# A banded attention, a SiLU feed-forward and a top-1 expert stage in one kernel: five small edits to the order of its work

## The chip, the cores and the metric

The kernel runs on one core of one Trainium2 chip. A core has TensorE (PE, with its weight loads shown apart as PEld), VectorE (DVE), ScalarE (ACT), GpSimd (POOL) and SyncE (SP, which here issues nearly all of the transfers). Each engine works through its own list of instructions in the order in which they stand, and waits where an instruction needs something that isn't there yet. The metric is the device time of one execution in microseconds (us); the figure that counts is the median of several runs.

## The reference

Three parts follow each other. Inputs are drawn at random; there are 2 x 768 = 1536 tokens of width 512.

```python
# attention: 2 batches, 8 heads, 768 positions, head width 64
scores = q @ k.T / 8 + bias            # bias = -slope[h] * distance
keep   = (col < n_global) | ((row - col >= 0) & (row - col < n_local))   # 8 and 96
a      = softmax(where(keep, scores, -1e9))
x      = a @ v                         # [1536, 512]
# feed-forward, width 2048
h = x @ w_in;  x = (h * sigmoid(h)) @ w_out
# experts: 8 of them, width 1024; each token goes to the one with the largest logit
e   = argmax(x @ w_gate)
out = softmax(..)[e] * sigmoid(x @ w_output_gate)[e] * (relu(x @ w1[e]) @ w2[e])
```

## The kernel before, in words

**Attention.** The tokens stand in 12 tiles of 128, and a slot `s` is one tile and one pair of heads (`n,hp=divmod(s,4)`). In the first 24 slots (`slot_b`, tiles 0 to 5) the scores of slot `s+1` are computed on PE (`emit_qk`, L174, tile `xy`), DVE adds the distance table `tabs` and takes the extreme (`emit_tb`, L184), ACT takes the exponential (L195), PE transposes the result (L214), DVE or ACT copies it out (L220), and PE multiplies it by v (`emit_px`, L231, tile `px`). After the four slots of a tile the reciprocal sums are spread over 512 columns (`rx`), turned on PE into a bank `rb` (`emit_rb`, L238), copied from there to `xn` by DVE (L242) and multiplied into `px` (L243); POOL then writes `xT`. The distance tables come from three DVE steps in `table` (L124, L125, L126) over columns 0 to 2 or column 3, and from `tab_heads` (L129, L130). Before the first scores PE runs idle products on a constant tile (`warm`, L84), four before the two limits `n_global` and `n_local` are spread by a small product (`spread`, L92) and four behind it.

**The second half of the attention** (`slot`, tiles 6 to 11) is interleaved with the feed-forward. It splits the exponentials into two half-precision parts; the lower part is a subtraction (`emit_l`, L202, tile `hl`), given to POOL for the head pairs in `LOPB` and to DVE for the one that isn't in it. In the slot with `hp==1` POOL also splits the tile's v (L154), and the lower part of head pair 0 is computed in that same slot.

**Feed-forward.** Two token groups `u` of 256 are done in the first pass (`c==0`), then one at a time. Each step `f` of 16 does `s1_mm` (L356, 12 products of 256 columns for a group), the activation on ACT and DVE (L360, L362, L365, L366), and, two steps late, `s2_mm` (L377 to L379). In the first pass each step also decodes and splits the weights for later steps: L304, L305, L306 on DVE, L328 on ACT, L334 and L340 on POOL. `s2_mm` of step 0 takes the four accumulator banks `s20` to `s23`, which until then were handed round by `abank`, for `rb` among others.

**Experts.** Each expert `p` has 8 steps `f`: `f1_mm` (L716, L717 or L722), `f1_ev`, some splits of the next expert's weights (`split_u`, L586 on ACT and L587 on DVE), and `f2_mm` two steps late (L744 to L751). The rows of the next expert are turned by `prep_x` (L706 on PE into `xm`, L708 on ACT and L709 on DVE into `xwT`), one tile of up to 128 rows a step, from step `PX=4` on; the second expert has three such tiles. `tail` (L697, L698) copies the factor and the token number of a row.

What sets the order is the code itself: `manual_schedule` keeps the instructions of each engine as they are written, and the rotation of banks and buffers adds the waits.

Of the kernel before, what the change touches and what calls it, by code (L numbers as in the profile page):

```python
# [10 lines left out]
F32 = mybir.dt.float32  # L11
# [5 lines left out]
AF = mybir.ActivationFunctionType  # L17
ALU = mybir.AluOpType
AX = mybir.AxisListType
P = 128  # L20
# [3 lines left out]
def kernel(ctx, tc, qk, v, n_global, n_local, w_in, w_out, wg, w1, w2, out):  # L24
# [6 lines left out]
    SB=24  # L31
# [4 lines left out]
    LS=3  # L36
    WL=6
    DQS=(9,10,11,13,15,17,18,19,21)
    LOPB=(1,2,3)
    WPL=(4,6,8,10,12,14,16,18,20)  # L40
    WPS=(12,18,22)
    const=ctx.enter_context(tc.tile_pool(name="const",bufs=1,side="left"))
# [1 line left out]
    attn=es_a.enter_context(tc.tile_pool(name="attn",bufs=1,side="right"))  # L44
# [29 lines left out]
    V=nc.vector; A=nc.scalar; G=nc.gpsimd; T=nc.tensor; S=nc.sync  # L74
# [6 lines left out]
    def warm(k):  # L81

        if not wm: wm.append(ps.tile([P,512],F32,tag="s1b",name="wm",bufs=1))
        for _ in range(k): T.matmul(wm[0].rearrange("p (a b) -> p a b",a=4),ones,ones[:,None,:].to_broadcast([P,4,P]),start=True,stop=True)  # L84
# [34 lines left out]
    def table(k,steps=(0,1,2)):  # L119

        w=tabm['w'][0]
        rel,col,loc,a=(w[:,i,k] for i in range(4))
        ng=pf[:,0:1]; nl=pf[:,2:3]
        if 0 in steps: V.tensor_scalar(out=loc,in0=rel,scalar1=nl,scalar2=BIG,op0=ALU.is_ge,op1=ALU.mult)  # L124
        if 1 in steps: V.scalar_tensor_tensor(out=loc,in0=col,scalar=ng,in1=loc,op0=ALU.is_ge,op1=ALU.mult)  # L125
        if 2 in steps: V.scalar_tensor_tensor(out=a,in0=rel,scalar=nl,in1=loc,op0=ALU.min,op1=ALU.add)  # L126
# [6 lines left out]
    def abank(shape,name):  # L133
        tg=atags[0][acnt[0]%len(atags[0])] if not ded[0] else 'a'; acnt[0]+=1
        return ps.tile(shape,F32,tag=tg,name=name,bufs=1)
# [64 lines left out]
    def emit_l(n,hp):  # L200
        t=tt.pop((n,hp)); x=hl.pop((n,hp)); nch=ce=1 if n%NT==0 else 2
        (G if hp in LOPB else V).tensor_tensor(out=x[:,:,1],in0=t[:,:,:ce],in1=x[:,:,0],op=ALU.subtract)  # L202
        y=attn.tile([P,2,2,nch,P],F16,tag="pT",name="pT",bufs=3)
# [29 lines left out]
    rb={}  # L233
    def emit_rb(n):

        r=rs.pop(n)
        m=abank([P,KC,P],"rb")
        for k in range(KC): T.transpose(m[:,k,:],r[:,k*P:(k+1)*P],ident)  # L238
        rb[n]=m
    def emit_xx(n):  # L240
        m=rb.pop(n); x=attn.tile([P,KC,P],F32,tag="t",name="xn",bufs=3)
        V.tensor_copy(x,m)  # L242
        V.tensor_tensor(out=x,in0=pvt[n],in1=x,op=ALU.mult)  # L243
        put_xt(n,x,G)
    def emit_pv(n,hp):
# [28 lines left out]
    def put_xt(n,m,e=None):  # L274
        c,u=divmod(n,2)
        if u==0: xT[c]=mp.tile([P,2,KC,256],F32R,tag="xT",name="xT",bufs=3)
        sl=xT[c][:,:,:,u*P:(u+1)*P]
        if e: e.tensor_copy(sl[:,0],m)
        else: A.activation(out=sl[:,0],in_=m,func=AF.Copy)
        (e or V).tensor_tensor(out=sl[:,1],in0=m,in1=sl[:,0],op=ALU.subtract)  # L280
# [341 lines left out]
    def late_split():  # L622
        xr=xrp[NTT//2-1]
        for t in range(2): ea['l',t]=halves(xr[:,t,:512],(G,V)[t])
# [21 lines left out]
    def early1(hf,part):  # L646
        if part==0: ea['t']=s1bank([P,512],"eh")
        t=ea['t']; x=ea['xT']
        for k in range(6*part,6*part+6):
            ww,xx=((0,0),(0,1),(1,0))[k//4]; kc=k%4  # L650
            T.matmul(t,x[:,xx,kc,:],uq[2*hf,kc][:,ww],start=(k==0),stop=(k==11))
        if part==0: return
        h=m2['a'].tile([P,512],F32,tag="eh",name="ehs",bufs=2); ea['h',hf]=h
        A.activation(out=h,in_=t,func=AF.Relu)
# [116 lines left out]
    def folds():  # L771
        while late: late.pop(0)()
# [12 lines left out]
    def moe2():  # L785
        late_split()
        early1(0,0)
        run_gates(2)
        early1(0,1)
        logits(NTT-2)  # L790
        early1(1,0)
        run_gates(1)
        late1()
        run_gates(1)
        early1(1,1)
        run_gates(1)
        early2(0)
        late3()
        order(1)
        moe2_open2()  # L800
        for k in range(NQR):
            load_u(4+k//4,k%4)
            if k==3: load_x(1)
        load_t(0)
        early3(0,0)
        early2(1)
        early3(0,1); early3(1,0)
        early3(1,1)
        early4()
        atags[0]=['s1','s1b','a','pv']  # L810
        LG=2
        steps=[(p,f) for p in range(NE) for f in range(8)]
        for g in range(len(steps)+LG):
            if g<len(steps):
                p,f=steps[g]
                def spl():
                    split_u(4*(p+1)+nq[1]//4,nq[1]%4,False); nq[1]+=1
                f1_mm(p,f)
                if f!=2: folds()
                if p+1<NE and f==0: nq[:]=[0 if p else NQR,0]  # L820
                ns=(0,0,3,3,3,3,2,2)[f] if p+1<NE else 0
                f1_ev(p,f,spl if ns else lambda: None)
                if p+1==NE and 2<=f<5: flags(f-2)
                if p+1<NE:
                    for _ in range(ns-1): spl()
                    while nq[0]<min(16,nq[1]+4*(f+1),nq[1]+NQR): load_u(4*(p+1)+nq[0]//4,nq[0]%4); nq[0]+=1
                    if p and f==0: load_x(p+1)
                    if p==0 and f==5:
                        for k,s,n in tiles(0): tail(0,k,xwt[0][:,k,0:1],xwt[0][:,k,1:2])
                    t=tiles(p+1)  # L830
                    px=PX
                    if px<=f<px+len(t): prep_x(p+1,t[f-px][0])
            if g>=LG:
                p2,f2=steps[g-LG]
                if p2<NE-1:
                    f2_mm(p2,f2)
                    if f2==7: f2_ev(p2)
                    continue
                big,last=tiles(p2)
                if f2==7: f2_mm(p2,0,[big])  # L840
                f2_mm(p2,f2,[last])
                if f2==7:
                    f2_ev(p2,[last])
                    for k in range(1,8):
                        f2_mm(p2,k,[big])
                        if k==2: folds()
                    f2_ev(p2,[big])
# [156 lines left out]
    def slot_b(s):  # L1004

        ev=[]
        n5,h5=divmod(s-LT-2,4); o5=0<=s-LT-2<SB
        n,hp=divmod(s,4); n1,h1=divmod(s-1,4); n3,h3=divmod(s-LT,4); n4,h4=divmod(s-LT-1,4)
        n2,h2=divmod(s-2,4); cur=s<SB; o1=0<=s-1<SB; o2=0<=s-2<SB; o3=0<=s-LT<SB; o4=0<=s-LT-1<SB
        def a_():  # L1010
            if s<SB-3: want(min(s+WL,SB-1))
            elif cur: want(s+3)
            if s==0:
                m=two()
                for j in range(2): emit_qk(n,hp,j,m)
            if cur: emit_tb(n,hp,0)
            if s+1<SB or o3: m=two()
            if o3: cp[0]=emit_tr(n3,h3,m)
            if s+1<SB:
                for j in range(2): emit_qk(*divmod(s+1,4),j,m)  # L1020
            if s<3: warm(2)
            if s>=SB and o3: emit_cp(*cp[0],V)
            if o1 and s<SB: emit_exp(n1,h1)
        ev.append(a_)
        def a2():
            if cur: emit_tb(n,hp,1)
            if o3 and s<SB: emit_cp(*cp[0],A if DQ<=s<23 else V)
            if o1 and s>=SB: emit_exp(n1,h1)
            if o4: emit_px(n4,h4)
            if o3 and h3==3 and own(n3): emit_rb(n3)  # L1030
            if o4 and h4==3 and not own(n4): emit_rb(n4)
            if o5 and h5==3 and not own(n5): emit_xx(n5)
            if o2 and h2==3:
                for k in range(2): emit_rs(n2,k)
                r=attn.tile([P,512],F32,tag="t",name="rx",bufs=3)
                G.tensor_copy(r.rearrange("p (h d) -> p h d",h=H),rs[n2].to_broadcast([P,H,D])); rs[n2]=r
        ev.append(a2)
        def b_():
            if cur: glob_k(n,hp)
            if h4==3 and o4 and own(n4): emit_xx(n4)  # L1040
            if s==0: table(slice(0,3),(1,))
            if s==1: table(slice(0,3),(2,))
            for d,h in TB.get(s,()): tab_heads(slice(0,2) if d==0 else slice(2,3),slice(0,2) if d==0 else slice(2,3),(h,))
            if hp==3 and 4*(n+1)<SB and cur: load_v(n+1)
        ev.append(b_)
        return ev
    cp=[None]
# [41 lines left out]
    with tc.manual_schedule():  # L1089
# [3 lines left out]
        warm(4)  # L1093
        table_floats(slice(3,4),V)
        spread()
        warm(4)
        table(slice(3,4))
        table_floats(slice(0,3),A)
        tab_heads(slice(3,4),slice(3,4),range(H))
        table(slice(0,3),(0,))  # L1100
        rows_init()
        s=0
        while s<SB:
# [12 lines left out]
        def run_gates(k):  # L1116
            for _ in range(min(k,len(gq))): gq.pop(0)()
        for g in range(len(steps)+LAG):
            live=g<len(steps)
            if live:  # L1120
                c,f=steps[g]
# [116 lines left out]
```

## Time and profile before

| | us |
|---|---|
| median of 3 runs | 564.19 (563.9 to 564.52) |
| profiled execution, its own time | 564.78 |
| span of the profiled execution | 563.0 |
| PE busy | 548.8 |
| DVE busy | 385.9 |
| ACT busy | 309.9 |
| POOL busy | 168.5 |

The span runs from the first to the last instruction, and 1.8 us of the profiled execution's time lie around it. Busy time says how long an engine had an instruction in work; a wait of PE shows as a hole in its rows, and in brackets behind the instruction that ends the hole stands its length and what released it. The chain of waits goes back from the last instruction to whatever released each step. A matmul row merges equal instructions that follow each other (x12: twelve of them), and its duration runs to the modelled end of the last, so that two rows that follow each other are better compared by their starts.

### The profile page before, as it was taken

The page shows a single profiled execution, that of the slowest core. Times are in us where ns is not written, and L with a number is a line of the kernel's source. Part 1 is how long each engine was busy: PE and PEld are TensorE (multiplying, and loading weights), DVE is VectorE, ACT ScalarE, POOL GpSimd, SP SyncE. Part 2 cuts the span into 40 slices and gives each one's busy share as a digit, 9 for nine tenths or more (in the row PEclk, how much of TensorE's full clock was granted, in tenths as well). Part 3 has the DMA queues.
Part 4 walks back from the last instruction along what each step waited for, and adds up shares of the span by engine and source line. Part 5 has one row for each costly group of instructions (what it writes and reads, how often), then busy time and mean ns, then how long its engine had stood idle before and what let it go on. Part 6 is the DMA issues. An engine that isn't in the chain of part 4 may idle for free.

```text
span 563.0 us, 12050 instructions
## 1 busy us (share of the span) xinstructions
PE 548.8 (97%) x4051; PEld 467.9 (83%) x4051; DVE 385.9 (69%) x1115; ACT 309.9 (55%) x823; POOL 168.5 (30%) x231
## 2 busy tenths in 40 slices
PE   8999899999999999999999999999999999999993
PEld 4668799998888888888999989889887888888881
DVE  6997888884588857565634458548674966977950
ACT  6993444442645565444623436627655776867740
POOL 4875977765141521232101010210011010010011
PEclk9999999999999999999999999999999999999997
DMA  7870887895575875854594259129673866867500
GB/s 224 280 252 17 297 264 238 259 315 177 180 177 143 189 195 138 194 154 124 119 179 128 80 161 368 72 74 349 218 223 134 269 219 225 263 215 270 159 20 23
DMA packets 87531, 106.76 MB, mean 190 GB/s; under 512 B 35980, under 2 KB 50316, under 8 KB 87460
## 3 DMA queue, kind: packets, MB, share of 16 engines
q1 hardware_dynamic: 84980, 99.25, 59.4%
q0 software_dynamic: 2192, 6.39, 3.0%
q8 instruction: 34, 0.56, 0.4%
q10 hardware_dynamic: 288, 0.26, 0.2%
q14 instruction: 37, 0.30, 0.2%
HBM read 87.14 MB, written 17.66 MB: 186 GB/s over the span
## 4 chain that ended last, share of the span: by engine, by line
PE 86%; DVE 6%; DMA 2%; ACT 2%; issue 1%; SPq 1%; POOL 0%; POOLq 0%; DVEq 0%; ACTq 0%
PE s L356 23%; PE s L377 8%; PE s L378 7%; PE s L379 7%; PE h L716 6%; PE y L749 4%; PE y L750 4%; PE y L751 4%; PE h L717 4%; PE xy L174 3%; PE pv L255 2%; PE h L722 2%; PE y L745 1%; PE y L744 1%; PE px L231 1%
## 5 line engine op out<-in xcount | busy, mean ns | idle before, releaser
L356 PE MATMUL s<-xT,wi 128*128 128x256 f32 x1152 | 152.5, 284 | 0.0
L356 PEld LDWEIGHTS s<-xT,wi 128*128 128x128 f32 x1152 | 147.2, 190 | 5.4 <-issue 0.3
L360 ACT ACTIVATE u<-s 128x256 f32<-128x256 f32 x96 | 36.4, 380 | 96.2 <-PE s L356 92.8
L377 PE MATMUL s<-woh,g 128*128 128x512 f32 x192 | 78.5, 409 | 1.6 <-DVE xn L242 1.6
L587 DVE TENSOR_TENSOR uq<-qr,uq 128x512 fp32r<-128x512 f32 x112 | 74.3, 689 | 3.1 <-ACT uq L586 1.1
L378 PE MATMUL s<-woh,g 128*128 128x512 f32 x192 | 75.7, 394 | 0.0
L586 ACT ACTIVATE uq<-qr 128x512 fp32r<-128x512 f32 x112 | 66.5, 625 | 0.7 <-DMA qr<-in_w_dram 0.7
L673 POOL DMA_INDIRECT out_dram<-y,ixt x17 | 18.9, 1111 | 155.6 <-ACT y L762 115.8
L362 DVE SCALAR_TENSOR_TENSOR s<-u,s 128x256 f32<-128x256 f32 x64 | 27.2, 425 | 54.7 <-ACT u L360 54.6
L195 ACT ACTIVATE t<-t,mx 128x256 f32<-128x256 f32 (+1 forms) x96 | 46.0, 485 | 0.5 <-DVE mx L184 0.5
L377 PEld LDWEIGHTS s<-woh,g 128*128 128x128 f32 x192 | 36.3, 189 | 8.8 <-DVE xn L242 2.0
L202 POOL TENSOR_TENSOR hl<-t,hl 128x512 f16<-128x512 f32 (+1 forms) x18 | 19.6, 1088 | 73.6 <-ACT g L365 32.1
L378 PEld LDWEIGHTS s<-woh,g 128*128 128x128 f32 x192 | 36.3, 189 | 5.0
L379 PE MATMUL s<-wolr,g 128*128 128x512 f32 x128 | 39.8, 392 | 0.0
L366 DVE TENSOR_TENSOR g<-s,g 128x256 fp32r<-128x256 f32 x64 | 26.9, 421 | 16.6 <-ACT g L365 14.8
L729 DVE TENSOR_TENSOR h<-h,hs 128x192 f32<-128x192 f32 (+5 forms) x56 | 20.8, 372 | 25.3 <-ACT hs L728 25.3
L365 ACT ACTIVATE g<-s 128x256 fp32r<-128x256 f32 x64 | 24.2, 378 | 23.0 <-DVE s L362 22.9
L749 PE MATMUL y<-uq,hh 128*128 128x512 f32 (+1 forms) x88 | 36.7, 417 | 0.0
L750 PE MATMUL y<-uq,hh 128*128 128x512 f32 (+1 forms) x88 | 34.6, 394 | 0.0
L751 PE MATMUL y<-uq,hh 128*128 128x512 f32 (+1 forms) x88 | 34.6, 393 | 0.0
L731 ACT ACTIVATE hh<-h 128x192 fp32r<-128x192 f32 (+5 forms) x56 | 19.7, 352 | 26.3 <-DVE h L729 15.8
L716 PE MATMUL h<-xwT,uq 128*128 128x448 f32 (+5 forms) x144 | 32.5, 347 | 0.0
(282 smaller groups left out, 1106.2 us busy)
## 6 DMA issues: line engine op xcount, KB each, us to landing
qr<-in_w_dram SPq DMA_DIRECT2D x128, 256.0 KB, 4.1
wolr<-wlo_d SPq DMA_DIRECT2D x64, 256.0 KB, 3.3
wiraw<-in_w_in_dram SPq DMA_DIRECT2D x16, 512.0 KB, 5.1
wraw<-in_w_out_dram SPq DMA_DIRECT2D x13, 512.0 KB, 3.7
ring<-in_qk_dram SPq DMA_DIRECT2D x22, 256.0 KB, 4.3
xe<-xe SPq DMA_DIRECT2D x7, 792.0 KB, 5.8
wlo_d<-wol SPq DMA_DIRECT2D x16, 256.0 KB, 2.9
xw<-xe SPq DMA_DIRECT2D x15, 264.0 KB, 4.7
```

Of the source, the lines that this page charges most:

```text
L195: A.activation(out=t[:,j,:ce],in_=t[:,j,:ce],func=AF.Exp,scale=-1.0 if 4*n<SB else 0.125,bias=mx[n][:,h:h+1],accum_out=ss[n][:,h,0:1])
L356: T.matmul(t,w[:,ww,kc,:],x[:,xx,kc,:],start=(k==0),stop=(k==11)); k+=1
L360: A.activation(out=u,in_=t,func=AF.Tanh,scale=0.5)
L377: T.matmul(o,g[u][:,0,sl],wh,start=(f==0),stop=False)
L378: T.matmul(o,g[u][:,1,sl],wh,start=False,stop=False)
L379: else: T.matmul(o,g[u][:,0,sl],wl,start=False,stop=(f==FB-1))
L586: A.activation(out=t[:,0],in_=r,func=AF.Copy)
L587: (G if (i%2 if pool is None else pool) else V).tensor_tensor(out=t[:,1],in0=r,in1=t[:,0],op=ALU.subtract)
L716: for kc in range(KC): T.matmul(t[:,:2*W],uq[4*p+2*(f//4),kc][:,0,s],xwT[p,kc][:,:,:W],start=(kc==0),stop=False)
L749: T.matmul(o,hi,w[:,0],start=(f==0),stop=False)
L750: T.matmul(o,g[:,z:z+n],w[:,0],start=False,stop=False)
L751: T.matmul(o,hi,w[:,1],start=False,stop=(f==7))
```

## The change

Five edits. The second run of idle products has one product where it had four. The first step of the tables of columns 0 to 2 (L124) moves from the place ahead of the first slot to the place behind the first slot's two score instructions. The copy of `rb` into `xn` for the last tile of the first half (tile 5) is done by ACT, and stands right behind the turns that fill `rb`; the other tiles keep theirs on DVE where it was. The lower parts of head pair 0 go to POOL and those of head pair 2 to DVE (`LOPB`). The second expert's rows are turned one step sooner, at steps 3, 4 and 5 of the first expert, and the two `tail` calls of the first expert move from step 5 to step 7.

```diff
-    LOPB=(1,2,3)
+    LOPB=(0,1,3)
...
         for k in range(KC): T.transpose(m[:,k,:],r[:,k*P:(k+1)*P],ident)
         rb[n]=m
+        if n==SB//4-1: rb_copy(n,A)
+    def rb_copy(n,e):
+        m=rb[n]; x=rb[n]=attn.tile([P,KC,P],F32,tag="t",name="xn",bufs=3)
+        if e is V: V.tensor_copy(x,m)
+        else: A.activation(out=x,in_=m,func=AF.Copy)
     def emit_xx(n):
-        m=rb.pop(n); x=attn.tile([P,KC,P],F32,tag="t",name="xn",bufs=3)
-        V.tensor_copy(x,m)
+        if n<SB//4-1: rb_copy(n,V)
+        x=rb.pop(n)
         V.tensor_tensor(out=x,in0=pvt[n],in1=x,op=ALU.mult)
         put_xt(n,x,G)
...
-                    if p==0 and f==5:
+                    if p==0 and f==7:
                         for k,s,n in tiles(0): tail(0,k,xwt[0][:,k,0:1],xwt[0][:,k,1:2])
                     t=tiles(p+1)
-                    px=PX
+                    px=PX if p else PX-1
                     if px<=f<px+len(t): prep_x(p+1,t[f-px][0])
...
-            if s==0: table(slice(0,3),(1,))
+            if s==0: table(slice(0,3),(0,1))
...
         spread()
-        warm(4)
+        warm(1)
         table(slice(3,4))
         table_floats(slice(0,3),A)
         tab_heads(slice(3,4),slice(3,4),range(H))
-        table(slice(0,3),(0,))
         rows_init()
```

On DVE at the program's start, from the tables of column 3 (`wk`) to the first scores of head pair 0 (L184, two instructions each with the read of the extreme into `mx`), this stood before:

```order
L126 SCALAR_TENSOR_TENSOR wk<-wk,pf 128x128
L129 TENSOR_SCALAR tabs<-wk 128x128 x2
L124 TENSOR_SCALAR wk<-wk,pf 128x384
L181 MEMSET ss 128x8
L184 ISA t,mx<-xy,tabs 128x128
L184 ISA mx 128x1
L125 SCALAR_TENSOR_TENSOR wk<-wk,pf 128x384
```

and this stands there now:

```order
L126 SCALAR_TENSOR_TENSOR wk<-wk,pf 128x128
L129 TENSOR_SCALAR tabs<-wk 128x128 x2
L181 MEMSET ss 128x8
L184 ISA t,mx<-xy,tabs 128x128
L184 ISA mx 128x1
L124 TENSOR_SCALAR wk<-wk,pf 128x384
L125 SCALAR_TENSOR_TENSOR wk<-wk,pf 128x384
```

The two score instructions of the first head pair (the second one and its read are left out in both) have moved ahead of the 384-column step.

On ACT around feed-forward step 1 (the activations of `s_950` and `s_963` are its two groups, `woh` and `wi` are weight parts for later products) this stood before:

```order
L360 ACTIVATE u<-s_950 128x256
L360 ACTIVATE u<-s_963 128x256
L365 ACTIVATE g<-u 128x256 x2
L328 ACTIVATE woh<-wt 128x512
L328 ACTIVATE wi<-wt 128x512
```

and this stands there now (the lines of the changed program are five higher):

```order
L365 ACTIVATE u<-s_947 128x256
L365 ACTIVATE u<-s_960 128x256
L370 ACTIVATE g<-u 128x256 x2
L244 ACTIVATE xn<-rb 128x512
L333 ACTIVATE woh<-wt 128x512
L333 ACTIVATE wi<-wt 128x512
```

The copy of `rb` stands between the step's activations and the next weight parts; on DVE the copy L242 is gone from its place behind a decode (L306) of the following step.

On ACT in steps 3 and 4 of the first expert (`uq` are split weights of the second expert, `xwT` its turned rows) this stood before:

```order
L728 ACTIVATE hs<-h_5614 128x192
L586 ACTIVATE uq<-qr 128x512
L731 ACTIVATE hh<-h_5614 128x192
L586 ACTIVATE uq<-qr 128x512 x2
L708 ACTIVATE xwT<-xm 128x4x128
L728 ACTIVATE hs<-h_5658 128x192
```

and this stands there now:

```order
L736 ACTIVATE hh<-h_5575 128x192
L591 ACTIVATE uq<-qr 128x512 x2
L713 ACTIVATE xwT<-xm 128x4x128
L733 ACTIVATE hs<-h_5621 128x192
L591 ACTIVATE uq<-qr 128x512
L736 ACTIVATE hh<-h_5621 128x192
```

`h_5614` and `h_5621` are the same step 4 in the two programs, and the first tile of turned rows stands ahead of its activations where it stood behind them.

## Rows read from the trace of the kernel before

**Rows 1.** Busy time by stretch: us in it, then each engine with instructions.
```profile
61.00:134.00 73.00, 73.00 (x470) 66.62 (x469) 60.19 (x102) 33.33 (x76) 54.42 (x81) 1.00 0.85 276
143.00:157.00 14.00, 13.86 (x123) 11.80 (x122) 9.86 (x35) 8.44 (x26) 3.10 (x3) 1.00 0.50 153
157.00:180.00 23.00, 22.52 (x211) 19.17 (x210) 18.49 (x75) 11.91 (x39) 7.33 (x9) 1.00 0.68 158
180.00:320.00 140.00, 140.00 (x1256) 123.82 (x1255) 81.55 (x270) 66.20 (x187) 31.93 (x31) 1.00 0.65 153
```

**Rows 2.** Chain of waits, first 45 us: start, us, engine, tile, line.
```profile
3.92 1.82 PE wm L84 x4
...
8.59 0.96 PE wm L84 x2
...
10.08 0.54 PE wm L84 x2
...
11.43 0.47 DVE pT L220 x2
...
19.50 5.73 DMA ring<-in_qk_dram
...
42.55 1.62 PE s L356 x12
```

**Rows 3.** Timeline of PE at three holes: start, us, what, [idle before, releaser].
```profile
56.95 0.40 PE L378 MATMUL s<-woh,g 128*128 128x512 f32 x1
58.95 0.50 PE L377 MATMUL s<-woh,g 128*128 128x512 f32 x1 [1.59 <-DVE xn L242]
59.28 0.39 PE L378 MATMUL s<-woh,g 128*128 128x512 f32 x1
59.51 0.39 PE L377 MATMUL s<-woh,g 128*128 128x512 f32 x1
...
65.61 1.07 PE L379 MATMUL s<-wol,g 128*128 128x512 f32 x4
...
169.30 0.66 PE L420 MATMUL gt<-ident,xr 128*128 128x128 f32 x4 [0.29 <-DVE gx L427]
...
396.24 0.39 PE L745 MATMUL y<-uq,hh 128*64 128x512 f32 x1
397.09 2.06 PE L722 MATMUL h<-xwT,uq 128*128 128x272 f32 x12 [0.46 <-ACT xwT L708]
...
400.14 1.66 PE L722 MATMUL h<-xwT,uq 128*128 128x272 f32 x12
```

**Rows 4.** Timeline of DVE at the start, same columns.
```profile
5.24 0.36 DVE L129 TENSOR_SCALAR tabs<-wk 128x128 bf16<-128x128 f32 x2
5.52 0.41 DVE L124 TENSOR_SCALAR wk<-wk,pf 128x384 f32<-128x384 f32 x1
...
6.49 0.29 DVE L184 CUSTOM_DVE_ANT_0 t<-xy,tabs 128x128 f32<-128x128 f32 x1 [0.54 <-PE xy L174]
```

**Rows 5.** Timeline of DVE, ACT and POOL around step 1, same columns.
```profile
58.21 0.68 DVE L242 COPY xn<-rb 128x512 f32<-128x512 f32 x1
...
53.44 0.63 ACT L328 ACTIVATE woh<-wt 128x512 fp32r<-128x512 f32 x1 [0.84 <-DVE wt L306]
...
61.70 1.29 POOL L340 TENSOR_TENSOR wol<-wt,woh 128x512 fp32r<-128x512 f32 x1
```

**Rows 6.** Instructions of L202 on DVE (ns min/median/max), then DVE and POOL at tile 7.
```profile
L202 DVE TENSOR_TENSOR hl<-t,hl x6: 692/980/2054, 150.8 to 265.1; 128x512 f16<-128x512 f32 x5, 128x256 f16<-128x256 f32 x1
...
166.19 2.02 DVE L202 TENSOR_TENSOR hl<-t,hl 128x512 f16<-128x512 f32 x1
...
166.47 1.19 POOL L154 TENSOR_TENSOR vpr<-vraw,vpr 128x512 bf16<-128x512 f32 x1
```

**Rows 7.** The second expert's rows: issue on SP, landing, and PE's place in step 3.
```profile
379.31 1.42 SPq L691 DMA_DIRECT2D xw<-xe  x3
...
DMA to landing us min/median/max: 4.7/4.9/5.2
...
384.36 0.59 PE L717 MATMUL h<-xw,qb 128*128 128x192 f32 x4
```

## The prediction, made before the changed kernel ran

> **What bounds the kernel now.** I read the busy time by stretch first. PE has work in 73.00 of 73.00 us of the feed-forward's first pass and in 140.00 of 140.00 from 180 to 320, and only between 143 and 180 a little is missing, 0.14 and 0.48; DVE and POOL stay below it everywhere, at 60.19 and 54.42 of 73.00 in the first pass [rows 1]. So the reader is to see a kernel in which PE's list of products is nearly the whole span, and in which a gain has to come from a hole in that list or from the head of the program, where there is no list to work on yet. Next I read the chain of waits for the first 45 us: PE's idle products, the copy of the first transposed exponentials, a ring transfer issued at 19.50 that takes 5.73, and then PE without a break up to the feed-forward at 42.55 [rows 2]. Last I read PE's timeline at its holes, and DVE, ACT and POOL beside them [rows 3 to 7].
>
> **The start (one idle product for four, L124 behind the first scores).** Four idle products took 1.82, so one takes 0.455 and three less take 1.36 off PE ahead of the first scores [rows 2]. DVE would have been free for the first scores at 5.52 + 0.41 = 5.93 and waited 0.54 for PE's `xy`, up to 6.49 [rows 4]. Without L124 it is free at 5.24 + 0.36 = 5.60, and PE's scores come at 6.49 - 1.36 = 5.13 or so; DVE is now the later one, and the scores are read 6.49 - 5.60 = 0.89 sooner. L124 is paid behind them, so that the tables that hang on L125 gain only 0.89 - 0.41 = 0.48. PE gains a little less than 1.36 too. A pair of idle products took 0.96 at 8.59 and 0.54 at 10.08 [rows 2]: there PE's granted clock rose from its low level, 1.2 GHz, to 2.4. If the rise stays at its moment, a pair that ran behind it now runs ahead of it and pays 0.42, which leaves 1.36 - 0.42 = 0.94. The first copy `pT` (11.43) hangs on all three, and the ring's transfer, PE at 25.2 and the feed-forward at 42.55 hang on that copy's chain. I expect what lies between 0.48 and 0.94 to get through: 0.7. Bounds: 0, if the transfer issued at 19.50 goes by something else, and 1.3, if the rise comes sooner by as much and nearly all of PE's 1.36 arrives.
>
> **The copy of `rb` on ACT.** PE starts a product at 56.95 and the next at 58.95, released by DVE's copy `xn`; where nothing waits, starts lie 59.51 - 59.28 = 0.23 apart. That is 2.00 - 0.23 = 1.77 lost, and the one behind starts 0.33 later where 0.23 would do, 0.10 more: 1.87, of which the bracket shows 1.59 [rows 3]. The product isn't short of data: it needs the bank that `rb` occupies until DVE has copied it out at 58.21 + 0.68 [rows 5]. ACT sits idle for 0.84 ahead of L328 at 53.44, and the copy lands there in its list. ACT's price for 128x512 out of such a bank isn't in these rows; the nearest are ACT's own 0.63 for L328 and DVE's 0.68 for the same copy [rows 5], both below 0.84, so it hides, and the bank is free some 4 us before it is wanted. If that cover were gone, L328 and the weight parts behind it in ACT's list would come up to 0.63 late. What is late next is POOL's `wol` (L340), ready at 61.70 + 1.29 = 62.99, which L379 reads at 65.61 [rows 3, 5]; moved up by 1.87 it reads at 63.74, 0.75 behind. POOL doesn't move with PE there, and with 54.42 of 73.00 [rows 1] it can catch up. I take 1.8; bounds 1.1 (the margin of 0.75 is used up) and 1.9.
>
> **Head pairs 0 and 2.** DVE's subtraction L202 takes 980 ns in the median, 692 at best and 2054 at worst. The worst stands at tile 7: 2.02 from 166.19, while POOL works on L154, 1.19 from 166.47 [rows 6]. Behind it in DVE's list stands L427, and PE's transposes of `gx` wait for that at 169.30 [rows 3]. With pair 0 on POOL the two stand in one list, 1.19 each by the row, and DVE is some 2.02 sooner at L427; pair 2's subtraction, now on DVE, falls into a slot without L154 and should take the 0.69 of the undisturbed ones. I price the edit by PE's missing time in the two stretches, 0.14 + 0.48 = 0.62 [rows 1], take 0.7, and set two things against each other: behind other holes PE loses more than the bracket shows (0.28 more behind the 1.59, and more behind the 0.46 below [rows 3]), but not every hole of these stretches need be this subtraction's. From 180 on DVE's 0.69 costs nothing, since PE has no hole there and DVE is busy 81.55 of 140.00 [rows 1]. Bounds: a gain of 1.1, and a loss of 0.3, if POOL's two pieces in a row make a transposed part late.
>
> In the Trainium skill, "SBUF — State Buffer", section "The single rule", puts such pairs down to an exclusive lock between DVE and GpSimd on a shared port: the loser doesn't slow down but blocks until the other is done. The 2.02 beside POOL's 1.19 fits that, 0.69 + 1.19 = 1.88 being near it [rows 6]. By that rule a further DVE instruction with two such inputs may meet POOL's L154 where L202 did, since L154 now stands later; the price would be POOL's 1.19 again, on DVE, and the sum by it is that of the first rival below where that instruction stands ahead of one that PE waits for.
>
> **The second expert's rows.** PE's block L722 waits for ACT's `xwT`. The product ahead of it starts at 396.24 and the block at 397.09: 0.85 - 0.23 = 0.62 lost; and the block takes 2.06 where a later one takes 1.66, 0.40 more because the last pieces still come in while it runs: 1.02 [rows 3]. One step sooner, the three tiles are turned before this hole, and about a step of PE's work lies between the last copy and its reader. That pays only if `xw` has landed. It is issued at 379.31 and takes 4.7 to 5.2, so the first tile is there at 384.0 to 384.5. Its place in PE's list is behind L717 of step 3, which starts at 384.36 and gives way to the next product about 0.42 later, at 384.8: 0.3 to 0.8 to spare [rows 7]. All four terms move PE and the issue alike. The copies on ACT and DVE are the same as before, a step earlier, and the two `tail` calls go to where the third tile's copy used to stand. I take 1.0; bounds 0 and 1.0, and a loss only if the landing is late by more than this, since PE would then stand at the transposes.
>
> **The sum.** 0.7 + 1.8 + 0.7 + 1.0 = 4.2. The profiled execution took 564.78 (563.0 of span and 1.8 around it): 560.6. It lies 0.59 over the median of 564.19, so the median to expect is 560.0, with 558.4 and 562.9 where all bounds fall on one side except those that are rivals below.
>
> **Rivals.**
> *The subtraction collides again.* Pair 2's L202 or the DVE instruction behind it meets a POOL piece, and PE's holes between 143 and 180 stay. For it: DVE has 18.49 of 23.00 to do there [rows 1], so little room. Against: POOL has 7.33. It gives 560.0 + 0.7 = 560.7.
> *Another wait takes the place of the big one, or the start is hidden.* If POOL's `wol` or a bank behind it gives 0.75 of the 1.8 back, or if the transfer at 19.50 doesn't come sooner, or both: 560.0 + 0.75 + 0.7 = 561.5.
> *The change doesn't do what it says.* The rows of the second expert aren't there in step 3, PE stands at L706 instead of at L722, and the start gains nothing: 560.0 + 1.0 + 0.7 = 561.7, and with the rival before added 563.1, no change that can be measured.
> *PE's clock rises late (slower).* Three idle products less are 1.36 less of work on an engine that is at 1.2 GHz until about 10 us [rows 2]. If the rise fails there, each stretch of PE's list that took 0.54 takes 0.96. While PE is waiting for others that costs nothing; from 25.2 to 42.55 it doesn't wait [rows 2], and each us at the low level loses 0.42 / 0.96 = 0.44. Up to 42.55 that is 17.3 x 0.44 = 7.6, and 560.0 + 7.6 = 567.6. It decides against the change from (4.2 + 1.1) / 0.44 = 12 us of such a delay on. Against it: between 8.59 and 25 PE has the same work as before, and one idle product ahead of it is still there.
>
> For this last one speaks the Trainium skill, "TensorE: Matmul & The Clock Gate", section "What's actually happening": "the default state is throttled, and activity releases the throttle". By that sentence less idle work can only put the rise off. The trace shows one rise, about 10 us in [rows 2], and no row shows what one product less does to it.
>
> **Chances.** Forecast with all four terms within their likely sizes 0.50 (its own range 559.2 to 560.8); one or two terms missing, as in the first two rivals and the first half of the third, 0.34; nearly all lost, 0.10; the late clock or another loss, 0.06. A measurement of this kernel tells 0.2%, 1.1 us, from no change: faster is below 563.1, slower above 565.3. The first two cases are faster, 0.84; same 0.10; slower 0.06. The range that holds 8 in 10 goes from 559.0, which is 1.0 more gain than the sum, to 562.6, which takes in every single miss and most pairs of them.
>
> **What would show it.** After the change the third product of step 0's output no longer waits for DVE's copy, and starts 0.23 behind the second; L379 starts with no POOL wait. The idle products still shorten from 0.96 to 0.54 a pair about 10 us in, and `pT` is copied at 10.5 to 11.0. DVE's L202 has no entry near 2 us, and PE's transposes L420 near 165 don't wait for L427. L722's first block starts 0.23 behind the last product and takes 1.66. The span should be 558.8. I'm wrong if PE has a new hole that is as long as one of these, or if the products from 25 us on run at the low level.

## The result, and the profile after

The changed kernel took 560.0 us (median of 4 runs, 559.37 to 560.28) beside 564.36 for the kernel before on the same chip (4 runs, 563.9 to 565.48): a ratio of 0.9918, 95% interval 0.9901 to 0.9935 (ratios here are formed from the runs, not from the two medians). The forecast was 560.0 in a range of 559.0 to 562.6. The profiled execution has a span of 558.5 where it had 563.0.

Where the 4.5 went is read by following single instructions through both traces. The first 12 products of the feed-forward stood at 42.55 [rows 2] and stand at 41.76 now; the products on `wol` (L379) at 65.61 [rows 3], now at 62.94; the transposes L420 at 169.30 [rows 3], now at 165.81; the second expert's second block at 400.14 [rows 3], now at 396.04. So PE's list is 0.79 early behind the start, 2.67 behind step 0, 3.49 at tile 7's transposes and 4.10 in the second expert. It stays there to POOL's last scatter, which was issued at 554.78 and now at 550.67; the 0.4 that are left of the span lie behind that issue, in the landing.

Busy time by stretch, for three of the four stretches of [rows 1]:

```profile
61.00:134.00 73.00, 73.00 (x465) 66.42 (x464) 59.53 (x100) 33.05 (x77) 54.61 (x81) 1.00 0.82 273
...
143.00:157.00 14.00, 14.00 (x129) 12.23 (x130) 10.97 (x48) 7.62 (x27) 2.95 (x4) 1.00 0.47 129
157.00:180.00 23.00, 23.00 (x233) 19.57 (x229) 17.80 (x70) 12.68 (x41) 8.34 (x9) 1.00 0.73 177
```

PE's 13.86 of 14.00 and 22.52 of 23.00 have become 14.00 and 23.00. PE's timeline after, at the places of [rows 3], all lines five higher:

```profile
56.17 0.39 PE L383 MATMUL s<-woh,g 128*128 128x512 f32 x1
56.41 0.39 PE L382 MATMUL s<-woh,g 128*128 128x512 f32 x1
...
62.94 1.07 PE L384 MATMUL s<-wol,g 128*128 128x512 f32 x4
...
165.81 0.60 PE L425 MATMUL gt<-ident,xr 128*128 128x128 f32 x4
...
381.71 0.63 PE L711 MATMUL xm<-ident,xw 128*128 128x128 f32 x4 [0.49 <-DMA xw<-xe]
...
393.16 0.39 PE L750 MATMUL y<-uq,hh 128*64 128x512 f32 x1
393.39 1.67 PE L727 MATMUL h<-xwT,uq 128*128 128x272 f32 x12
```

The third product stands 0.24 behind the second, where it stood 2.00 behind; L425 has no wait in front; the second expert's first block starts 0.23 behind the product ahead of it and takes 1.67 where it took 2.06. What is new is the wait of 0.49 for `xw` at 381.71. The chain of waits shows one that has grown, at the start: the ring's transfer is issued 2.50 sooner than in [rows 2] but takes 7.42 in place of 5.73, and PE waits 0.90 for it where it waited 0.25:

```profile
17.00 7.42 DMA ring<-in_qk_dram
...
24.47 0.70 PE xy L174 x4
...
41.76 1.62 PE s L361 x12
```

DVE at the start, and ACT's copy (answering to [rows 4, 5]):

```profile
5.18 0.36 DVE L129 TENSOR_SCALAR tabs<-wk 128x128 bf16<-128x128 f32 x2
...
5.56 0.29 DVE L184 CUSTOM_DVE_ANT_0 t<-xy,tabs 128x128 f32<-128x128 f32 x1
...
5.98 0.42 DVE L124 TENSOR_SCALAR wk<-wk,pf 128x384 f32<-128x384 f32 x1
...
9.95 0.49 DVE L220 COPY pT<-xy 128x128 f32<-128x128 f32 x2 [0.67 <-PE xy L214]
```
```profile
52.03 0.60 ACT L244 ACTIVATE xn<-rb 128x512 f32<-128x512 f32 x1 [0.22 <-PE rb L238]
52.66 0.63 ACT L333 ACTIVATE woh<-wt 128x512 fp32r<-128x512 f32 x1
```

### The profile page after: what moved, and what is told of

The parts are those of the page before. It is cut to its first block, busy times and chain, and to the rows that moved or that the text cites. A ratio compares the mean times of both kernels' runs of the same rounds, so it can differ in the third digit from the quotient of the medians.

```text
span 558.5 us, 12047 instructions
## 1 busy us (share of the span) xinstructions
PE 546.4 (98%) x4048; PEld 467.8 (84%) x4048; DVE 379.7 (68%) x1114; ACT 310.2 (56%) x824; POOL 168.2 (30%) x231
## 4 chain that ended last, share of the span: by engine, by line
PE 91%; DMA 2%; POOL 1%; issue 1%; SPq 1%; DVE 1%; ACT 0%; POOLq 0%
PE s L361 25%; PE s L382 8%; PE s L383 8%; PE s L384 8%; PE h L721 7%; PE y L754 4%; PE h L722 4%; PE y L756 4%; PE y L755 4%; PE xy L174 3%; PE pv L260 2%; PE h L727 2%; PE y L750 2%; PE y L749 2%; PE px L231 1%
## 5 line engine op out<-in xcount | busy, mean ns | idle before, releaser
L202 POOL TENSOR_TENSOR hl<-t,hl 128x512 f16<-128x512 f32 (+1 forms) x18 | 19.6, 1086 | 85.5 <-ACT g L370 37.6
```

## The experiments

All start from the changed kernel. The time of a single run says little at this size: 17 to 27 runs of the kernel before, in each of the three sets, lie between 561.86 and 567.22. So each kernel is also read by its profile in two pieces: where the feed-forward's first 12 products start (the head), and how much of the span lies behind that (the rest). The three columns that matter:

| kernel | median, ratio to before [95%] | head | rest |
|---|---|---|---|
| before | 564.4 to 564.7 | 42.55 | 520.4 |
| changed | 560.0, 0.9918 [0.9901, 0.9935] | 41.76 | 516.7 |
| changed, again | 560.64, 0.9931 [0.9915, 0.9947] | 41.97 | 517.2 |
| copy on DVE | 561.93, 0.9946 [0.9929, 0.9962] | 42.00 | 519.0 |
| old lower parts | 561.23, 0.9949 [0.9930, 0.9969] | 40.51 | 519.0 |
| turns a step later | 561.51, 0.9940 [0.9920, 0.9960] | 41.54 | 517.8 |
| old start | 560.94, 0.9928 [0.9904, 0.9952] | 42.28 | 516.8 |

Five profiles with the changed kernel's steps behind the start (its own two, the old start, and the two other idle counts below) have a rest of 516.7 to 517.2. Part of that agreement is luck: followed instruction by instruction, the changed kernel's second profile loses 0.5 against the first near 195 and 0.5 between 339 and 356, and saves 0.65 at `xw`. So a difference in that column is read together with the place in PE's list where it arises. Each kernel has one profile, the changed one two.

**Copy on DVE.**
```
-        if n==SB//4-1: rb_copy(n,A)
-        if n<SB//4-1: rb_copy(n,V)
+        rb_copy(n,V)
```


> The changed kernel with one edit undone: tile 5's copy of rb into xn is DVE's again, behind the step's decode. Theory (each edit pays the shift that PE's list shows at its place, start 0.8, copy 1.9, lower parts 1.2, second expert's rows 0.4): PE waits again for DVE's copy at the third product of the second token group's step 0, bracket about 1.6, two starts 2.0 apart, and everything behind comes 1.9 later; time 561.9. Rival (another wait would have stood there in its place anyway, POOL's wol or a bank): 560.5 to 561.0.


Measured: the hole is back, as long as the one of [rows 3] (1.60 beside 1.59, the two starts 2.00 apart). PE's timeline in this kernel:

```profile
56.41 0.40 PE L382 MATMUL s<-woh,g 128*128 128x512 f32 x1
58.41 0.50 PE L381 MATMUL s<-woh,g 128*128 128x512 f32 x1 [1.60 <-DVE xn L242]
58.75 0.40 PE L382 MATMUL s<-woh,g 128*128 128x512 f32 x1
```

The rest grows by about 2.1, of which 1.9 is this hole; a wait of 0.6 on `pT` near 197 is told of below. The median of 561.93 is the 561.9 expected. The theory holds and POOL's `wol` was no obstacle.

**Old lower parts.** `LOPB=(1,2,3)` again.


> The changed kernel with one edit undone: lower parts of head pair 0 on DVE and of pair 2 on POOL again. Theory: DVE's subtraction at tile 7 takes about 2.0 again beside POOL's L154, the three holes of PE between 140 and 175 come back (0.30, 0.45 and 0.36 by starts), time 561.2. Rival (only the brackets of the two stretches count): 560.6. Rival (the holes went because PE's list came earlier by the other edits): 560.0.


Measured: DVE's subtraction at tile 7, what POOL did beside it, and the hole on PE that follows:

```profile
162.11 2.15 DVE L202 TENSOR_TENSOR hl<-t,hl 128x512 f16<-128x512 f32 x1
```
```profile
161.50 0.99 POOL L523 DMA_INDIRECT xe<-xr,gdi  x1 [0.90 <-DMA xe<-xr,gdi]
162.52 1.18 POOL L154 TENSOR_TENSOR vpr<-vraw,vpr 128x512 bf16<-128x512 f32 x1
```
```profile
165.34 0.66 PE L425 MATMUL gt<-ident,xr 128*128 128x128 f32 x4 [0.42 <-DVE gx L432]
```

All three holes between 140 and 175 are back, and PE's list loses 1.2 in them against the changed kernel's first profile, as expected. The rest grows by more, 1.9 to 2.3, through 0.5 near 195 and 0.9 between 339 and 356. Those aren't charged to the edit: the unaltered kernel's second profile loses 0.5 at each of the two places, and the last lower part is done by 286, well ahead of the second one. That the holes went because of the other edits is excluded.

**Turns a step later.**
```
-                    if p==0 and f==7:
+                    if p==0 and f==5:
-                    px=PX if p else PX-1
+                    px=PX
```


> The changed kernel with one edit undone: the second expert's rows are turned at steps 4, 5 and 6 again and the tail copies stand at step 5. Theory: the edit gives 1.02 at the block behind and loses 0.64 in the wait for the landing of xw, so undoing it costs 0.4: time 560.4, with no wait at the transposes of xw and the old wait of about 0.5 ahead of the first block on xwT. Rival (the prediction's term): 561.0.


Measured: no wait at the transposes, and the old one at the block:

```profile
392.79 0.39 PE L750 MATMUL y<-uq,hh 128*64 128x512 f32 x1
393.47 2.05 PE L727 MATMUL h<-xwT,uq 128*128 128x272 f32 x12 [0.28 <-ACT xwT L713]
...
396.50 1.68 PE L727 MATMUL h<-xwT,uq 128*128 128x272 f32 x12
```

The median of 561.51 lies above both expected times. Here the hole is worth (0.68 - 0.23) + (2.05 - 1.68) = 0.82, and the rest grows by 0.7 to 1.1: nearer to the prediction's 1.0 than to the 0.4 that the first profile of the changed kernel shows. The changed kernel's second profile, below, gives the reason.

**Old start.** `warm(4)`, and L124 ahead of the first slot.


> The changed kernel with two edits undone: four idle products again ahead of the first scores, and L124 ahead of them. Theory: PE reaches the ring's product near 25 us 1.46 later and waits 0.25 there in place of 0.9, so 0.8 net: time 560.8. Rival (the transfer alone sets it and its issue does not move): 560.0. Rival (all of the 1.46 counts): 561.5.


Measured: the head comes 0.3 to 0.5 later than in the two profiles of the changed kernel, the ring wait is 0.2, the median isn't told from the changed kernel's (ratios 0.9928 and 0.9918 or 0.9931). Not settled by this run; see below.

**The changed kernel again.**


> The changed kernel once more, unaltered, for a second profile and for times beside those of the three below. Theory: two of its waits are chance. The wait of 0.9 for the ring transfer at 24.47 and that of 0.5 for xw at 381.7 need not come back; pT's first copy lies anywhere from 9.4 to 10.9, as in the three kernels that share this start; time 559.5 to 561. Rival (both waits belong to the change): they come back within 0.2.


Measured: the wait for `xw` is gone (landing 4.9 in place of 6.2), that for the ring is 0.7, and a third one has come. From the waits of PE (waited for: us in total, times, longest):

```profile
PE xy L174 <- DMA ring<-in_qk_dram: 0.7, 1, 0.7
PE pv L260 <- DMA pT<-hl: 0.5, 1, 0.5
```

Half of the theory: the `xw` wait is chance, since no other kernel with these turns has it either. Without it, the second expert's rows give what was forecast: the step's first product on `xw`, at 383.66 in the kernel before, stands at 381.06 here, 2.60 early, and the second block at 396.49, 3.65 early, a gain of 1.05 between them. The ring's wait comes and goes: of nine profiles with one idle product or none and the clearing of the rows in its place, four have 0.7 to 0.9 of it, the others 0.2 or nothing. The wait on `pT` near 195 stands in nearly all profiles but the first two, the one with the old lower parts included (0.2 there), so it isn't charged to that edit.

**The subtraction beside POOL, first try.** Old lower parts, and `split_v2` in the slot with `hp` 0:
```
-            if hp==0 and n<NTT: split_v1(n)
-            if hp==1 and n<NTT: split_v2(n)
+            if hp==0 and n<NTT: split_v1(n); split_v2(n)
```


> The changed kernel with head pair 0's lower parts on DVE and pair 2's on POOL again, but with POOL's L154 (and its ACT half) moved one slot sooner, to the slot with hp 0, out of the way of DVE's subtraction. Theory (the subtraction is slow because POOL works beside it): DVE's subtraction at tile 7 takes 0.7 in place of 2.0, the hole ahead of the transposes near 165 is gone, and the time is that of the changed kernel, 560 to 560.5. Rival (DVE has no room for any subtraction there): it takes 0.7, but a hole of 0.3 or more stays near 165, time 561. Rival (it is slow by itself, at this size): 2.0 again.


Measured: 563.82 (0.9989 [0.9978, 1.0]), outside every expectation. The subtraction takes 693 ns at most, so it is POOL's company that makes it slow. But PE has more holes than before, up to 0.9, and one of 0.54 near 165 as well, because ACT now stands at L153 until POOL has done L150, with an activation that DVE and PE need queued behind it. At 228 it looks so:

```profile
228.24 0.63 ACT L153 ACTIVATE vpr<-vraw 128x512 bf16<-128x512 f32 x1 [3.37 <-POOL vraw L150]
228.78 0.36 ACT L370 ACTIVATE g<-s 128x256 fp32r<-128x256 f32 x1
```

So this kernel has a side effect of its own, and it answers neither for the hole near 165 nor for the time; the next one is without that side effect.

**Second try.** Old lower parts, and POOL's L154 alone one slot later:
```
-        G.tensor_tensor(out=t[:,2],in0=r,in1=t[:,1],op=ALU.subtract)
+        vlo[n]=r
...
+    def split_v3(n):
+        G.tensor_tensor(out=vpr[:,n%3][:,2],in0=vlo.pop(n),in1=vpr[:,n%3][:,1],op=ALU.subtract)
...
+            if hp==2 and n<NTT: split_v3(n)
```


> The changed kernel with head pair 0's lower parts on DVE and pair 2's on POOL again, and POOL's L154 alone one slot later (ACT's list stays as it is, which was not so in the kernel that moved it a slot sooner and in which ACT waited for POOL). Theory (POOL's work beside it is what makes DVE's subtraction slow, and that is the whole of the edit's gain): the subtraction takes 0.7 at tile 7, no hole near 165, and the time is the changed kernel's, 560.0 to 560.7. Rival (the subtraction's mere presence ahead of the transposes' input costs too): 0.7, with a hole of 0.2 or more left near 165, 561. Rival (two pieces of POOL now meet in the later slot and PE waits for a transposed part): 561 or more with a wait on pT.


Measured: the subtraction (L205 here) at 0.69 everywhere (0.42 for the half-size first one), and PE without a wait ahead of the transposes that follow the subtraction (L428; lines are three higher in this kernel). Their input, DVE's L435 here, is ready at 166.1, 0.9 ahead of them:

```profile
L205 DVE TENSOR_TENSOR hl<-t,hl x6: 424/693/694, 148.5 to 264.2; 128x512 f16<-128x512 f32 x5, 128x256 f16<-128x256 f32 x1
```
```profile
165.41 0.68 DVE L435 TENSOR_TENSOR gx<-gt,gx 128x512 f32<-128x512 f32 x1
```
```profile
167.04 0.60 PE L428 MATMUL gt<-ident,xr 128*128 128x128 f32 x4
```
```profile
PE pv L263 <- POOL vpr L157: 2.9, 3, 1.6
```

That settles the cause of the hole near 165: the subtraction is slow because POOL's L154 works beside it, and at 0.69 it does no harm to the transposes. (PE's waits further up lend DVE no time here: the run of DVE instructions that the subtraction stands in starts 1.08 ahead of the row of transposes before these, in this kernel as in the one with the old lower parts.) The time is no answer to it, 562.97 (0.9982 [0.9967, 0.9998]), since the moved piece is now late for PE's products with `v`, three waits with 2.9 together.

**Four idle products, L124 late.** `warm(4)` alone.


> The changed kernel with four idle products again, while L124 stays behind the first scores. Theory (PE sets the first scores then, and a clock that rises by chance moves the rest): first scores at about 6.4, pT's first copy between 11.0 and 11.5, the ring wait below 0.3, first product of the feed-forward 0 to 1.5 later than in the changed kernel, time 560.5 to 561.3. Rival (the idle products cost nothing since DVE's tables are late anyway): first scores at 5.6.


**No idle product there.** `warm(1)` taken out.


> The changed kernel with no idle product left between the spread limits and the first scores. Theory (DVE's tables, not PE, are last ahead of the first scores by now, and the clock's rise is chance within a us or two): DVE's first scores stay at about 5.5, pT's first copy lies between 9.3 and 11, time 560 to 561, as in the changed kernel. Rival (less idle work puts the clock's rise off): the pairs of idle products are all at 1.0, the rise comes behind 11, time 561 or more.


Measured: 559.64 (0.9925 [0.9905, 0.9946]) and 559.51 (0.9925 [0.9903, 0.9946]), heads of 42.61 and 42.05. Both times lie below what was expected, and with four products PE still waited 0.4 for the ring. DVE's first scores, of the one with four and then of the one with none:

```profile
6.46 0.29 DVE L184 CUSTOM_DVE_ANT_0 t<-xy,tabs 128x128 f32<-128x128 f32 x1 [0.87 <-PE xy L174]
```
```profile
5.59 0.29 DVE L184 CUSTOM_DVE_ANT_0 t<-xy,tabs 128x128 f32<-128x128 f32 x1
```

So with L124 late the first scores come 0.87 to 0.90 sooner with one idle product or none than with four. L124's move by itself leaves them at 6.46, where they stood at 6.49, since PE is last there; with one product or none DVE's tables are last. But what lies behind depends on the clock. Idle pairs of two kernels with the same start (old lower parts, turns a step later):

```profile
5.29 1.04 PE L84 MATMUL wm<-ones 128*128 128x512 bf16 x2
6.99 0.62 PE L84 MATMUL wm<-ones 128*128 128x512 bf16 x2
7.97 0.60 PE L84 MATMUL wm<-ones 128*128 128x512 bf16 x2
```
```profile
5.47 1.03 PE L84 MATMUL wm<-ones 128*128 128x512 bf16 x2
7.17 1.03 PE L84 MATMUL wm<-ones 128*128 128x512 bf16 x2
8.86 1.04 PE L84 MATMUL wm<-ones 128*128 128x512 bf16 x2
```

In the one the trace's clock record goes to its high level, 2.4 GHz, at 7.07 us; in the other at 9.96, and all three pairs still run at 1.2. `pT`'s first copy lies at 9.36 and 10.73 there. Over the eight profiles that share this start it lies between 9.36 and 10.87, and the head between 40.46 and 42.30, mean 41.41; with four idle products, in three profiles, the head is 42.28 to 42.61, mean 42.48. The start's edits are thus worth about 1.1 in the profiles, with 1.8 between the best and the worst of the same start. The medians don't show it: four idle products took as long as none beside each other, and the old start keeps all of the gain that the medians can tell (0.9928). What the two edits of the start are worth in the median stays open.

**Clearing later; turns behind the second products; both.**
```
-            if s==6: rows_clear(0)
+            if s==16: rows_clear(0)
```
```
-                    if px<=f<px+len(t): prep_x(p+1,t[f-px][0])
+                    if p and px<=f<px+len(t): prep_x(p+1,t[f-px][0])
...
                     f2_mm(p2,f2)
+                    if g<8 and px<=f<px+len(t): prep_x(1,t[f-px][0])
```


> The changed kernel with the clearing of the first expert's rows (792 KB, ahead of the ring transfers in SP's list near 14 us) issued ten slots later. Theory (the ring transfer that PE waits for at 24 us is late because of what is queued ahead of it): it lands some 2 us sooner, no wait on the ring, PE's list from 24 us on comes 0 to 1.0 sooner than in the changed kernel, by how early the clock rose; time 559.3 to 560. Rival (the transfer's own duration or its issue sets it): the wait stays as it is, 560.0. Rival (the later place collides with the weight parts or the next ring transfers): a new wait between 28 and 45, 560.5 to 562.

> The changed kernel with the turns of the second expert's rows behind the second products of steps 3 to 5 in place of ahead of them. Theory (the first tile's place in PE's list came before its landing in the profile): the transposes stand 1.2 later in the list, the wait is gone whether the landing takes 4.6 or 6.2, and the first block on xwT still does not wait; time 559.4 to 560. Rival (landing moves with the issue and the wait is chance): no difference, 560.0. Rival (the copies now come too late for the next expert): a wait of 0.3 or more ahead of the block, 560.3.

> The changed kernel with both moves that its profile suggests: the clearing of the first expert's rows ten slots later, and the turns of the second expert's rows behind the second products of steps 3 to 5. Theory: no wait on the ring at 24 us, none on xw, time 559.3 to 560.0, which is 0.4 to 0.9 below the changed kernel beside it in these runs (560.2 to 560.6). Rival (both waits were chance): the changed kernel's time.


Measured: 559.77 (0.9917 [0.9902, 0.9932]) with the clearing later, 560.19 (0.9929 [0.9913, 0.9945]) with the turns behind, 559.66 (0.9928 [0.9908, 0.9948]) with both. The wait for the ring is gone in both kernels that clear later, one with a late clock (`pT` 10.82, head 41.58) and one with an early clock (`pT` 9.83, head 40.59). The changed kernel had `pT` at 9.95 and its head at 41.76. But with the clearing in its old place and `pT` at 9.76 (the turns behind, alone) the head was 40.72 and there was no wait of note either, so that the transfer queued ahead causes the wait fits these profiles and isn't shown by them. The turns behind the second products save only the chance wait. That the version with both beats the changed kernel isn't shown: the intervals overlap, and the two idle counts beside it have the same median.

## Why the prediction was right, point by point

**The copy of `rb`**, 1.8 of 4.2: right in mechanism and size. 65.61 - 62.94 = 2.67, less 0.79 of the start, is 1.88. The copy took 0.60 on ACT, inside the 0.84 of idle time that was to cover it. POOL moved with PE after all: its L345 is done at 61.75, 1.24 sooner, and 62.94 needed it, a margin of 1.19 where 0.75 was forecast. `xn`'s multiplication on DVE, which POOL's work there hangs on, came 1.56 sooner (57.43 for 58.99).

```profile
60.46 1.29 POOL L345 TENSOR_TENSOR wol<-wt,woh 128x512 fp32r<-128x512 f32 x1
```

**Head pairs 0 and 2**, 0.7: right in mechanism, too small. From 2.67 to 3.49 at the transposes it is 0.82, and with a third hole behind them, at 176.62, PE is 3.90 early at 180. That makes 1.2, and undone the edit costs 1.2 at the same places. The prediction priced the three holes by their brackets (0.14, 0.29 and 0.20, together its 0.62); by starts they were worth 0.30, 0.45 and 0.36, the difference that it had itself measured at the two other holes. The cause of the hole at the transposes is shown by the second try. DVE's subtraction after, all six, where [rows 6] had a median of 980 and a worst of 2054:

```profile
L202 DVE TENSOR_TENSOR hl<-t,hl x6: 426/692/695, 155.0 to 274.3; 128x512 f16<-128x512 f32 x5, 128x256 f16<-128x256 f32 x1
```

The first rival was right that another instruction would meet L154, but not in the price: the later one is DVE's L435, which took 0.83 once where it takes 0.69, beside POOL's L154 from 164.33, and no one waited for it. The sizes follow one pattern. Wherever the subtraction or L435 met L154, DVE ended 0.54 to 0.56 behind L154's end, if L154 had more than 0.2 left: 168.21 behind 167.66 in [rows 6], 164.26 behind 163.70 with the old lower parts, 166.04 behind 165.49 at L435; with 256 columns in place of 512 it was 0.28. So L435 lost little because little of L154 was left when it came.

What the Trainium skill says in "SBUF — State Buffer", section "Who interferes with whom" (its "single rule"), that the loser blocks until the other is done, agrees with these ends. Its order does not: by that section the order of issue decides who blocks, and by the profile's starts, which are rough on POOL, the subtraction was first by 0.28 and 0.41 and lost all the same. So the prediction's "fits that" holds for the size and not for who blocks.

**The second expert's rows**, 1.0: right at the place, and wrong in the margin in the first profile. Behind the block the list is 4.10 early where it was 3.7 ahead of the turns (0.2 of the 3.90 was given back by then without a wait that the profile shows), so only 0.4 arrived there. The step that missed is the landing: the prediction took 4.7 to 5.2 from one profile as the range, and it was 6.2 here. That range was misread besides: the line in [rows 7] covers five transfers, the third expert's among them; of these rows it holds one landing, the first tile's 4.7, and the 5.2 is the third expert's. In later profiles it was between 4.5 and 5.5 with no wait; the second profile gains 1.05 there, and undoing the edit costs 0.82 by starts; the moved `tail` copies were not tried alone. The bound, and the third rival with its stand at the transposes, named the case, but not its chance. The prediction's own sign of being wrong, a new hole as long as one of the old ones, was met by this wait (0.49 beside the 0.46 that went), in one execution. The landing of the second expert's rows after:

```profile
DMA to landing us min/median/max: 6.2/6.2/6.2
```

**The start**, 0.7: 0.79 in this profile, by another way than worked out. The first scores came 0.93 sooner, 0.89 was forecast. But the prediction let the clock's rise stay at its moment; the trace's clock record has it at 9.75 before and at 8.06 here, so `pT` was copied 1.46 sooner, and the ring's transfer then took 0.65 of that back (a wait of 0.90 for one of 0.25). Two errors of a size met: that this term came out is luck. Where the rise did stay, the working holds: with it at 9.68 (second try) and 9.96 (turns a step later) `pT` is copied at 10.67 and 10.73, 0.7 sooner and inside the 10.5 to 11.0 forecast. Over more profiles the rise itself moves by more than the edit is worth.

**The rivals.** The late clock did not come: with one idle product `pT`'s first copy came 0.5 to 2.0 sooner than the 11.4 of before in every profile, and with none at all it lay at 10.26, among the others. By the clock records the rise lay at 9.29 to 9.75 in the three profiles with four idle products, at 9.52 with none, and anywhere from 7.07 to 10.39 in the ten with one. The prediction let three products less only put the rise off, from "the default state is throttled, and activity releases the throttle" in the Trainium skill ("TensorE: Matmul & The Clock Gate", "What's actually happening"); the runs show no such trend, and seven of the ten rises came sooner than the 9.75 of before. The other wait in place of the big one did not come either.

Two figures of the prediction don't follow from its terms. The four upper bounds, 1.3, 1.9, 1.1 and 1.0, give 558.9 and not 558.4, and the lower ones, with the loss of 0.3 left out as a rival's, 563.1 and not 562.9. And the third rival with the second added counts the start's 0.7 twice: without that it is 562.5 and not 563.1. The forecast and its range don't hang on either.

So the sum of 4.2 met 4.5 in the profile and 4.4 in the medians, with the lower parts 0.5 better, the expert's rows 0.6 worse in that one execution, 0.2 given back ahead of them, and 0.4 from the landing at the end, which no step of the change explains. Single terms missed by more than the sum did, and that they offset each other is luck.

## What to carry to other kernels

Where PE's list is the span, price an edit by the starts around the hole, not by the bracket: 1.59 of wait was 1.87 of list, 0.46 was 1.02. Follow one instruction through both traces to see which term was paid, and split the span at a fixed place, but read a difference in the pieces by where it arises: the rest repeated within 0.5 in five profiles whose heads differed by 0.9, in part because chance waits offset each other. A margin against a transfer's landing needs more than one execution behind it.

## What was not expected of the hardware

The rise of PE's granted clock at the start of a program is not at a fixed moment: with the same instructions ahead of it, it lay at 7.07 us in one execution and at 9.96 in another, and `pT`'s first copy came 1.4 later there.

And a DVE subtraction that began 0.28 and 0.41 ahead of POOL's L154 still took 2.02 and 2.15 in place of 0.69, although it was the first of the two to start. POOL had an indirect DMA in work until just then, but that isn't the cause: in the kernel of the second try the subtraction met an equal DMA, for the 0.29 that it still ran, without L154 behind it, and took 0.69.

```profile
186.27 0.69 DVE L205 TENSOR_TENSOR hl<-t,hl 128x512 f16<-128x512 f32 x1
```
```profile
185.57 0.99 POOL L526 DMA_INDIRECT xe<-xr,gdi  x1 [0.62 <-POOL xr L520]
```
